# Attention over a key/value window plus a gated feed-forward block: block transposes written in order, strided reading by TensorE, masks and gathers put off by a tile

## The chip, the cores and the metric

The kernel runs on one core of a Trainium2 chip. The metric is the time of the whole kernel on the device in microseconds (us), the median of several runs. A core has TensorE (matrix products, written PE in the profile, its weight loads PEld), VectorE (DVE), ScalarE (ACT), GpSimd (POOL) and SyncE (SP), which here issues the large loads. Data lie in SBUF, an on-chip memory of 128 partitions, and matrix products land in PSUM.

## The reference

For two sequences (B = 2) of one new token each, the kernel normalises the token x and adds three things: x, attention over the last W = 4096 keys and values of a cache, and a feed-forward block with a rectified gate. All data are float32.

```python
W = min(4096, max(256, Sk // 4))                 # Sk = 32768
q = (xn @ wq).reshape(B, Sq, Hq, Dh)...          # Hq = 32 query heads, Dh = 128
k = repeat(k_cache[:, :, Sk - W:, :], rep)       # 8 key/value heads, rep = 4
scores = einsum("bhqd,bhkd->bhqk", q, k) * (Dh ** -0.5)
o = einsum("bhqk,bhkd->bhqd", softmax(scores), v)
attention = o.reshape(B, Sq, Hq * Dh) @ wo
gate, up = xn @ W_gate, xn @ W_up                # 512 x 1792 each
block = ((gate * (gate > 0)) * up) @ W_down
return x + attention + block
```

Each key and each value is used by four query heads only, so the work is mostly moving 95 MB from memory and bringing the keys into a shape that TensorE can multiply.

## The kernel before

**Tiles.** The 16 pairs of sequence and key/value head are worked on in four rows of heads (g = 0 to 3, the loop at the end of the planned part), each in two tiles (a = 0, 1). A tile is one 4 MB load of 128 partitions: two heads, 64 partitions each, with 64 keys of 128 numbers in every partition. Keys arrive as `k`, values as `v`. All large loads go through one ring of four buffers of 4 MB (`RING`, `load`), and SyncE issues them in the order of the code. A load waits until the tile that held its buffer four loads earlier has been used up, and every load behind it in SyncE's queue waits with it. The order of loads is wq (2), w_gate, w_up, the keys of row 0, and then, for g = 1 to 3 and a = 0, 1, the keys of (g, a) and the values of (g - 1, a); at the end the values of row 3, w_down and wo.

**Order of the work.** Nothing is planned by a program: every engine works in the order in which the code issues its instructions, and waits there for what it needs. While row g is scored, the values of row g - 1 are multiplied.

- `scores(g, a, kt_in)`: VectorE turns the keys so that the 128 numbers of a key lie along partitions. It transposes blocks of 32 x 32 within a tile, four instructions of 128 x 2048 elements for each tile of keys, two for each half s1 of the tile, written to a `kT` tile. There are two `kT` buffers. A block transpose leaves two heads interleaved in every 32 columns (index h), and the kernel before lets VectorE separate them: in the stream of results h runs fastest, while in `kT` [CB, 2, JH, KL] the two values of h lie 512 floats apart. TensorE then multiplies a 32-column strip of the queries `qz` with 512 columns of `kT`, one matmul for each of four groups of 32 numbers (cb) and each h; the output `s` has four strips of 32 partitions, one for each pair of s1 and h.
- `maxima(g)` (second tile only): the largest score of each head, over VectorE, a transpose on TensorE (`mt`), VectorE, and a matmul (`nm_ps`) that spreads it again to `nm`.
- `softmax`: ScalarE's exponential `p` with row sums `l`. `turn`: two matmuls `pp` permute `p`, VectorE transposes it to `pt`, and the reciprocals `rl` of the sums are made.
- `values(g, a, v)`: 16 matmuls in four strips give `o`; VectorE multiplies `o` with a mask (`on`), since only some of its blocks are wanted.
- `gather(g, a)`: one matmul collects the wanted heads in `oa`. `finish(g)`: VectorE sums (`su`) and scales (`osb`). `spread_heads(r)`: eight matmuls `op` and a copy to `oT` bring the heads of two rows into the shape for the last product.

After the rows come the values of row 3, then the products with w_down and wo (`y`, `y_ps`) and the output `yo`. Ahead of the rows stand the normalisation, the queries (`q_ps`, `qt`, `rq`, `qz`) and the gate (`g_ps`, `u_ps`, `hh`, `hT`).

Of the kernel before, what the change touches and what calls it, by code (L numbers as in the profile page):

```python
# [9 lines left out]
F32 = mybir.dt.float32  # L10
AF = mybir.ActivationFunctionType
ALU = mybir.AluOpType
# [8 lines left out]
def kernel(  # L21
# [13 lines left out]
    P = 128  # L35
    B, _, D = x.shape
    _, HKV, SK, DH = k_cache.shape
# [12 lines left out]
    S1 = W // (Q * 512)  # L50
    L = 32
    PB = P // L
    CB = DH // L
# [9 lines left out]
    ktp = ctx.enter_context(tc.tile_pool(name="ktp", bufs=2))  # L63
# [36 lines left out]
    def load_kv(cache, name, g, a):  # L100
        r, b = divmod(g, B)
        base = cache[b, r * C + a, SK - W:SK, :]
        run = J * DH
        src = bass.AP(
            tensor=cache.tensor, offset=base.offset, ap=[[run, PK], [NP * SK * DH, 2], [1, run]]
        )
        return load(f"{name}{g}_{a}", src, [P, run])
# [20 lines left out]
    qz = const.tile([P, NG, CB, 2, ZW], F32, name="qz")  # L128
# [26 lines left out]
    mask = const.tile([P, 4], F32, name="mask")  # L155
# [52 lines left out]
    for kc in range(KC):  # L208
        m, k = divmod(kc, 2)
# [17 lines left out]
    for r in range(R):  # L227
# [15 lines left out]
        for b in range(B):  # L243
            for pb in range(PB):
                rows = slice(L * pb, L * pb + L)
                for a in range(NP):
                    lo = 2 * a * 16 + pb * REP
# [33 lines left out]
    JH = J // S1  # L281
    KL = L // 2
    ss, pts, rls = {}, {}, {}
    osb, ons, oa = {}, {}, {}

    def scores(g, a, kt_in):
        if a == 0:
            ss[g] = ps_s.tile([P, 512], F32, name=f"s{g}", tag="s")
        for s1 in range(S1):
            kt = ktp.tile([P, CB, 2, JH, KL], F32, name=f"kT{g}_{a}_{s1}", tag="kT")  # L290
            for n in range(2):
                lo = JH // 2 * n
                j = JH * s1 + lo
                nc.vector.transpose(  # L294
                    kt[:, :, :, lo:lo + JH // 2, :].rearrange("p c h j k -> p j c k h"),
                    kt_in[:, j * DH:(j + JH // 2) * DH],
                )
            for cb in range(CB):
                for h in range(2):
                    lo = 32 * (2 * s1 + h)  # L300
                    nc.tensor.matmul(  # L301
                        ss[g][lo:lo + 32, :], qz[:, g, cb, h, 16 * a:16 * a + 32],
                        kt[:, cb, h].rearrange("p j k -> p (j k)"),
                        start=(a == 0 and cb == 0), stop=(a == NP - 1 and cb == CB - 1),
                    )

    def maxima(g):

        m = work.tile([P, 1], F32, name=f"m{g}", tag="m")
        nc.vector.tensor_reduce(out=m, in_=ss[g], op=ALU.max, axis=AX.X)  # L310
        mt = ps_1.tile([1, P], F32, name=f"mt{g}", tag="misc")
        nc.tensor.transpose(mt, m, ident)
        mx = work.tile([1, C, REP], F32, name=f"mx{g}", tag="mx")
        nc.vector.tensor_reduce(
            out=mx, in_=mt.rearrange("p (s x b i) -> p x i s b", s=S1, x=C, b=PB), op=ALU.max, axis=AX.XY
        )
        mb = work.tile([1, S1, C, PB, REP], F32, name=f"mb{g}", tag="mb")
        for s1 in range(S1):
            nc.vector.tensor_scalar(
                mb[:, s1], mx[:, :, None, :].to_broadcast([1, C, PB, REP]), -SCALE, None, op0=ALU.mult  # L320
            )
        nm_ps = ps_1.tile([P, 1], F32, name=f"nm_ps{g}", tag="misc")
        nc.tensor.matmul(nm_ps, mb.rearrange("p s x b i -> p (s x b i)"), ones, start=True, stop=True)
        nm = work.tile([P, 1], F32, name=f"nm{g}", tag="nm")
        nc.vector.tensor_copy(nm, nm_ps)  # L325
        return nm

    def softmax(g, nm):
        p = work.tile([P, 512], F32, name=f"p{g}", tag="p", bufs=1)
        l = work.tile([P, 1], F32, name=f"l{g}", tag="l")  # L330
        nc.scalar.activation(p, ss[g], AF.Exp, bias=nm, scale=SCALE, accum_out=l)  # L331
        return p, l

    def turn(g, p, l):
        pp = ps_kt.tile([P, 2, 512], F32, name=f"pp{g}", tag="kt")
        for h in range(2):
            nc.tensor.matmul(pp[:, h], perm[:, h], p, start=True, stop=True)  # L337
        pts[g] = work.tile([P, NP * S1, JH, HK], F32, name=f"pt{g}", tag="pt")
        nc.vector.transpose(pts[g].rearrange("p n j k -> p j n k"), pp.rearrange("p h y -> p y h"))  # L339
        lp = ps_1.tile([HR, 1], F32, name=f"lp{g}", tag="misc")  # L340
        nc.tensor.matmul(lp, by_h.rearrange("p x i -> p (x i)"), l, start=True, stop=True)
        rls[g] = work.tile([HR, 1], F32, name=f"rl{g}", tag="rl")
        nc.vector.reciprocal(rls[g], lp)

    def values(g, a, v):
        o = ps_1.tile([P, 512], F32, name=f"o{g}_{a}", tag="o")
        for s1 in range(S1):
            for jh in range(2):
                for q in range(Q):
                    j = 16 * jh + 4 * q  # L350
                    lo = (JH * s1 + j) * DH
                    nc.tensor.matmul(  # L352
                        o[32 * q:32 * q + 32, :], pts[g][:, a * S1 + s1, j:j + 4, :].rearrange("p u k -> p (u k)"), v[:, lo:lo + 512],
                        start=(s1 == 0 and jh == 0), stop=(s1 == S1 - 1 and jh == 1),
                    )
        ons[a] = work.tile([P, 4, P], F32, name=f"on{g}_{a}", tag="on")
        nc.vector.tensor_tensor(  # L357
            ons[a], o.rearrange("p (u d) -> p u d", u=4), mask[:, :, None].to_broadcast([P, 4, P]), op=ALU.mult
        )

    def gather(g, a):

        if a == 0:
            oa[g] = ps_1.tile([HR, 4, P], F32, name=f"oa{g}", tag="oa")
        nc.tensor.matmul(  # L365
            oa[g], picks[:, a].rearrange("p h a i -> p (h a i)"), ons[a], start=(a == 0), stop=(a == NP - 1)
        )

    def finish(g):
        r, b = divmod(g, B)  # L370
        if b == 0:
            osb[r] = const.tile([HR, B, P], F32, name=f"osb{r}")
        su = work.tile([HR, P], F32, name=f"su{g}", tag="su", bufs=1)
        nc.vector.tensor_reduce(out=su, in_=oa[g].rearrange("h u d -> h d u"), op=ALU.add, axis=AX.X)  # L374
        nc.vector.tensor_scalar(osb[r][:, b], su, rls[g], None, op0=ALU.mult)

    def spread_heads(r):
        op = ps_1.tile([P, NJ, B], F32, name=f"op{r}", tag="misc")
        for e in range(NE):
            nc.tensor.matmul(  # L380
                op, spread[:, e].rearrange("h k e -> h (k e)"),
                osb[r][:, :, e * NJ:(e + 1) * NJ].rearrange("h b j -> h j b"),
                start=(e == 0), stop=(e == NE - 1),
            )
        nc.vector.tensor_copy(oT[:, r, :, :, 0], op)

    for g in range(NG):
        for a in range(NP):
            kt_in = load_kv(k_cache, "k", g, a)
            v_in = load_kv(v_cache, "v", g - 1, a) if g else None  # L390
            scores(g, a, kt_in)
            nm = maxima(g) if a else None
            if g:
                values(g - 1, a, v_in)
            pl = softmax(g, nm) if a else None
            if g:
                gather(g - 1, a)
                if a:
                    finish(g - 1)
                elif g % B == 1 and g > 1:  # L400
                    spread_heads((g - 2) // B)
            if a:
                turn(g, *pl)
    g = NG - 1
    vin = [load_kv(v_cache, "v", g, a) for a in range(NP)]
    dw = load_down()
# [28 lines left out]
    for a in range(NP):  # L435
        values(g, a, vin[a])
        gather(g, a)
# [48 lines left out]
```

## Time and profile before

| | |
|---|---|
| median of 3 runs | 278.11 us (277.75 to 278.12) |
| profiled execution | 277.64 us, span 275.9 us |
| TensorE busy | 166.6 us (60%), 948 records |
| VectorE busy | 147.2 us (53%), 121 instructions |
| ScalarE, GpSimd busy | 8.3 us, 8.1 us |
| read from memory | 94.90 MB, 344 GB/s over the span |
| mean granted TensorE clock | 0.85 |

The profile is of one execution. The span is the time between its first and last instruction. A row of a group of instructions names line, engine, operation, output<-inputs and count, then the busy time in us with the mean length in ns, and after the second bar the idle time of the engine before them with what ended it. The chain is the sequence of work that ended last, followed back from the end: its pieces give start, length and what was done ("issue" is a short time in which nothing shown was waited for). A row of a window gives for each engine its busy time and instructions, then the granted clock as a share of full speed, the busy share of the DMA engines and GB/s. A float32 matmul appears as two records.

### The profile page before, as it was taken

To read this page: it belongs to the slowest core of one execution; us is meant where nothing else is said; L and a number is where in the kernel's file an instruction comes from. 1 tells how busy PE (TensorE), PEld (TensorE's weight loads), DVE (VectorE), ACT (ScalarE), POOL (GpSimd) and SP (SyncE) were. 2 spreads that over 40 slices of the span, in tenths; PEclk is the share of its full clock that TensorE was granted. 3 is DMA by queue.
4 is the path that set the end of the run, shared out by engine and by line. 5 is a ranking of instruction groups with operands and counts; after the bars stand their busy time and mean duration, and the time that the engine had idled before them with its cause. 6 is when DMAs were issued, how large, how long until landed. Compare 5 with 4: busy or idle time off the path is not lost.

```text
span 275.9 us, 2205 instructions
## 1 busy us (share of the span) xinstructions
PE 166.6 (60%) x948; PEld 51.7 (19%) x948; DVE 147.2 (53%) x121; ACT 8.3 (3%) x27; POOL 8.1 (3%) x31
## 2 busy tenths in 40 slices
PE   0049759158476079547642981777089617768894
PEld 0042342111111012011110120122012301212242
DVE  1030123899952993695269729923991398241201
ACT  0010112000001000000100000010000000100000
POOL 8200000000000000000000000000000000000000
PEclk9999968859898559959995797799759957999999
DMA  7999999999999905996996289799907992999940
GB/s 304 456 404 451 399 451 420 456 418 418 450 423 413 456 14 219 404 442 249 437 394 290 76 378 442 323 380 375 432 29 287 399 451 102 391 363 399 393 186 1
DMA packets 3784, 95.03 MB, mean 344 GB/s; under 512 B 438, under 2 KB 448, under 8 KB 704
## 3 DMA queue, kind: packets, MB, share of 16 engines
q1 hardware_dynamic: 3756, 94.90, 82.2%
q8 instruction: 7, 0.11, 0.2%
q14 instruction: 1, 0.01, 0.0%
q10 hardware_dynamic: 20, 0.00, 0.0%
HBM read 94.90 MB, written 0.00 MB: 344 GB/s over the span
## 4 chain that ended last, share of the span: by engine, by line
DVE 48%; PE 41%; issue 6%; POOL 3%; ACT 1%; POOLq 0%; ACTq 0%
DVE kT L294 40%; PE o L352 10%; PE s L301 9%; PE q_ps L221 3%; PE pp L337 3%; PE y L424 3%; PE oa L365 2%; DVE pt L339 2%; PE g_ps L258 2%; DVE on L357 2%; PE op L380 1%; PE xt_ps L211 1%; PE u_ps L258 1%; PE rq L239 1%; DVE m L310 1%
## 5 line engine op out<-in xcount | busy, mean ns | idle before, releaser
L301 PE MATMUL s<-kT,qz 128*32 128x512 f32 x256 | 77.3, 760 | 66.1 <-DVE kT L294 66.1
L294 DVE STREAM_TRANSPOSE kT<-k 128x2048 f32<-128x2048 f32 x32 | 115.6, 3722 | 0.0
L301 PEld LDWEIGHTS s<-kT,qz 128*32 128x32 f32 x256 | 16.5, 134 | 122.7 <-DVE kT L294 77.7
L352 PE MATMUL o<-v,pt 128*32 128x512 f32 x256 | 34.8, 595 | 0.0
L357 DVE TENSOR_TENSOR on<-o,mask 128x512 f32<-128x512 f32 x8 | 5.5, 692 | 40.4 <-PE o L352 40.4
L211 PE MATMUL xt_ps<-rep,xn 2*128 2x32 f32 x16 | 3.7, 400 | 17.4 <-DVE xn L205 17.4
L352 PEld LDWEIGHTS o<-v,pt 128*32 128x32 f32 x256 | 9.1, 109 | 16.6 <-issue 16.6
L365 PE MATMUL oa<-on,picks 128*16 128x512 f32 x16 | 8.3, 597 | 6.5 <-DVE on L357 6.5
L310 DVE TENSOR_REDUCE m<-s 128x1 f32<-128x512 f32 x4 | 2.8, 692 | 14.9 <-PE s L301 14.9
L337 PE MATMUL pp<-p,perm 128*128 128x512 f32 x16 | 9.1, 699 | 1.2 <-ACT p L331 1.2
L221 PE MATMUL q_ps<-wq,xnT 128*32 128x512 f32 x64 | 9.2, 738 | 0.5 <-DVE xnT L213 0.5
L339 DVE STREAM_TRANSPOSE pt<-pp 128x1024 f32<-128x1024 f32 x4 | 5.0, 1250 | 7.0 <-PE pp L337 7.0
L331 ACT ACTIVATE p<-s,nm 128x512 f32<-128x512 f32 x4 | 2.7, 687 | 191.8 <-DVE nm L325 191.8
L188 DVE BATCH_NORM_STATS2 stats<-x 2x6 f32<-2x512 f32 x1 | 0.7, 682 | 11.6 <-DMA x<-in_A_x_dram 11.6
L211 PEld LDWEIGHTS xt_ps<-rep,xn 2*128 2x128 f32 x16 | 3.6, 319 | 17.4 <-issue 17.4
L248 DVE COPY qz<-rq 32x32 f32<-32x32 f32 x16 | 3.0, 187 | 7.1 <-ACT qz L248 7.1
L236 DVE COPY qT<-qt 128x32 f32<-128x32 f32 x2 | 0.4, 192 | 11.1 <-PE qt L232 11.1
L424 PE MATMUL y<-wo,oT 128*32 128x512 f32 x48 | 5.4, 594 | 0.0
L374 DVE TENSOR_REDUCE su<-oa 16x128 f32<-16x512 f32 x4 | 2.7, 679 | 4.5 <-PE oa L365 4.5
L258 PE MATMUL g_ps<-wg,xnT 128*32 128x448 f32 x32 | 4.5, 717 | 0.0
L424 PE MATMUL y<-wd,hT 128*32 128x512 f32 x28 | 4.5, 595 | 0.0
L232 PE MATMUL qt<-ident,qs 128*128 128x128 f32 x8 | 1.7, 357 | 4.4 <-DVE qs L229 4.4
(79 smaller groups left out, 67.9 us busy)
## 6 DMA issues: line engine op xcount, KB each, us to landing
k<-in_A_k_cache_dram SPq DMA_DIRECT2D x8, 4096.0 KB, 17.7
v<-in_A_v_cache_dram SPq DMA_DIRECT2D x8, 4096.0 KB, 16.7
wq<-in_A_wq_dram SPq DMA_DIRECT2D x2, 4096.0 KB, 16.8
wo<-in_A_wo_dram SPq DMA_DIRECT2D x1, 4096.0 KB
wg<-in_B_W_gate_dram SPq DMA_DIRECT2D x1, 3584.0 KB
wu<-in_B_W_up_dram SPq DMA_DIRECT2D x1, 3584.0 KB
wd<-in_B_W_down_dram SPq DMA_DIRECT2D x1, 3584.0 KB, 10.9
wo<-in_A_wo_dram SPq DMA_DIRECT2D x1, 2048.0 KB
```

What stands on the lines that cost most here:

```text
L211: nc.tensor.matmul(xt_ps[:, o, kc, :], cols, rep.rearrange("r s b -> r (s b)"), start=True, stop=True)
L221: nc.tensor.matmul(q_ps[r][32 * c:32 * c + 32, :], xnT[:, 0, kc, :], wqt[kc // 2][:, kc % 2, n * 512:(n + 1) * 512], start=(kc == 0), stop ...
L258: nc.tensor.matmul(dst[32 * c:32 * c + 32, :], xnT[:, 1, kc, :], wt[:, kc, c * MQ:(c + 1) * MQ], start=(kc == 0), stop=(kc == KC - 1),)
L294: nc.vector.transpose(kt[:, :, :, lo:lo + JH // 2, :].rearrange("p c h j k -> p j c k h"), kt_in[:, j * DH:(j + JH // 2) * DH],)
L301: nc.tensor.matmul(ss[g][lo:lo + 32, :], qz[:, g, cb, h, 16 * a:16 * a + 32], kt[:, cb, h].rearrange("p j k -> p (j k)"), start=(a == 0 an ...
L310: nc.vector.tensor_reduce(out=m, in_=ss[g], op=ALU.max, axis=AX.X)
L337: nc.tensor.matmul(pp[:, h], perm[:, h], p, start=True, stop=True)
L339: nc.vector.transpose(pts[g].rearrange("p n j k -> p j n k"), pp.rearrange("p h y -> p y h"))
L352: nc.tensor.matmul(o[32 * q:32 * q + 32, :], pts[g][:, a * S1 + s1, j:j + 4, :].rearrange("p u k -> p (u k)"), v[:, lo:lo + 512], start=(s ...
L357: nc.vector.tensor_tensor(ons[a], o.rearrange("p (u d) -> p u d", u=4), mask[:, :, None].to_broadcast([P, 4, P]), op=ALU.mult)
L365: nc.tensor.matmul(oa[g], picks[:, a].rearrange("p h a i -> p (h a i)"), ons[a], start=(a == 0), stop=(a == NP - 1))
L424: nc.tensor.matmul(y4[32 * t:32 * t + 32, :], lhsT.rearrange("p b s -> p (b s)"), w, start=(i < Q), stop=(i >= EARLY - Q))
```

## The change

Four things change in the functions of the rows.

1. `kT` is now [JH, CB, KL, 2], the order in which the transpose delivers its results, so VectorE writes one float behind the other. The heads stay interleaved, and the matmuls read every second float of `kT` (`kts[s1][:, :, cb, :, h]`).
2. The matmuls of a tile of keys are issued after both halves have been transposed, with the halves s1 inside the loop over cb: four strips in turn where there were two. Both `kT` buffers are therefore held until the 16 matmuls are nearly over.
3. The mask moves from `values` into `gather`, and `gather`, `finish` and `spread_heads` go to a list `late`, which is worked off in the next tile of keys, behind the transposes of its first half.
4. Exponential and `turn` come ahead of `values` in the second tile of a row.

```diff
-            kt = ktp.tile([P, CB, 2, JH, KL], F32, name=f"kT{g}_{a}_{s1}", tag="kT")
+            kt = ktp.tile([P, JH, CB, KL, 2], F32, name=f"kT{g}_{a}_{s1}", tag="kT")
+            kts.append(kt)
             for n in range(2):
...
                 nc.vector.transpose(
-                    kt[:, :, :, lo:lo + JH // 2, :].rearrange("p c h j k -> p j c k h"),
+                    kt[:, lo:lo + JH // 2].rearrange("p j c k h -> p (j c k h)"),
                     kt_in[:, j * DH:(j + JH // 2) * DH],
                 )
-            for cb in range(CB):
+            while late:
+                late.pop(0)()
+        for cb in range(CB):
+            for s1 in range(S1):
                 for h in range(2):
                     lo = 32 * (2 * s1 + h)
                     nc.tensor.matmul(
-                        ss[g][lo:lo + 32, :], qz[:, g, cb, h, 16 * a:16 * a + 32],
-                        kt[:, cb, h].rearrange("p j k -> p (j k)"),
+                        ss[g][lo:lo + 32, :], qz[:, g, cb, h, 16 * a:16 * a + 32], kts[s1][:, :, cb, :, h],
...
-        ons[a] = work.tile([P, 4, P], F32, name=f"on{g}_{a}", tag="on")
-        nc.vector.tensor_tensor(
-            ons[a], o.rearrange("p (u d) -> p u d", u=4), mask[:, :, None].to_broadcast([P, 4, P]), op=ALU.mult
-        )
-
-    def gather(g, a):
+        os[a] = o
+
+    def gather(g, a):
+
+        ons[a] = work.tile([P, 4, P], F32, name=f"on{g}_{a}", tag="on")
+        nc.vector.tensor_tensor(
+            ons[a], os[a].rearrange("p (u d) -> p u d", u=4), mask[:, :, None].to_broadcast([P, 4, P]), op=ALU.mult
+        )
...
             scores(g, a, kt_in)
-            nm = maxima(g) if a else None
+            if a:
+                turn(g, *softmax(g, maxima(g)))
             if g:
                 values(g - 1, a, v_in)
-            pl = softmax(g, nm) if a else None
-            if g:
-                gather(g - 1, a)
+                late.append(lambda g=g, a=a: gather(g - 1, a))
                 if a:
-                    finish(g - 1)
+                    late.append(lambda g=g: finish(g - 1))
                 elif g % B == 1 and g > 1:
-                    spread_heads((g - 2) // B)
-            if a:
-                turn(g, *pl)
+                    late.append(lambda g=g: spread_heads((g - 2) // B))
+    while late:
+        late.pop(0)()
```

Two places in the order of instructions show it. First VectorE, from the end of row 1 to the first mask of row 2; `kT_0_0` is the half s1 = 0 of tile a = 0, `on_1` the mask product of the second tile of the row before. Before:

```order
L325 COPY nm_483<-nm_ps_481 128x1
L357 TENSOR_TENSOR on_1_502<-o_1_485,mask 128x512
L374 TENSOR_REDUCE su_509<-oa_444 16x128
L375 TENSOR_SCALAR osb_508<-su_509,rl_396 16x128
L339 STREAM_TRANSPOSE pt_515<-pp_512 128x32x4x8
L343 RECIPROCAL rl_519<-lp_517 16x1
L294 STREAM_TRANSPOSE kT_0_0_526<-k_0_521 128x16x4x16x2 x2
L294 STREAM_TRANSPOSE kT_0_1_537<-k_0_521 128x16x4x16x2 x2
L357 TENSOR_TENSOR on_0_565<-o_0_548,mask 128x512
```

And after the change:

```order
L331 COPY nm_483<-nm_ps_481 128x1
L345 STREAM_TRANSPOSE pt_491<-pp_488 128x32x4x8
L349 RECIPROCAL rl_495<-lp_493 16x1
L298 STREAM_TRANSPOSE kT_0_0_519<-k_0_514 128x2048 x2
L367 TENSOR_TENSOR on_1_522<-o_1_497,mask 128x512
L382 TENSOR_REDUCE su_526<-oa_451 16x128
L383 TENSOR_SCALAR osb_525<-su_526,rl_396 16x128
L298 STREAM_TRANSPOSE kT_0_1_529<-k_0_514 128x2048 x2
L298 STREAM_TRANSPOSE kT_1_0_569<-k_1_565 128x2048 x2
```

The mask and the head sum of row 0 have moved from ahead of `pt` to between the two halves of the next tile of keys, and the first mask of row 2's tile has moved on by half a tile.

Second TensorE, the same stretch: the end of row 1 and the first tile of row 2. Before:

```order
L323 MATMUL nm_ps_481<-ones,mb_478 128x1
L352 MATMUL o_1_485<-v_1_448,pt_392 32x512 x16
L365 MATMUL oa_444<-on_1_502,picks 16x512
L337 MATMUL pp_512<-p_504,perm 128x512 x2
L341 MATMUL lp_517<-l_505,by_h 16x1
L301 MATMUL s_525<-kT_0_0_526,qz 32x512 x8
L301 MATMUL s_525<-kT_0_1_537,qz 32x512 x8
L352 MATMUL o_0_548<-v_0_523,pt_515 32x512 x16
```

And after the change:

```order
L329 MATMUL nm_ps_481<-ones,mb_478 128x1
L343 MATMUL pp_488<-p_485,perm 128x512 x2
L347 MATMUL lp_493<-l_486,by_h 16x1
L358 MATMUL o_1_497<-v_1_444,pt_392 32x512 x16
L373 MATMUL oa_451<-on_1_522,picks 16x512
L308 MATMUL s_518<-kT_0_0_519,qz 32x512 x2
L308 MATMUL s_518<-kT_0_1_529,qz 32x512 x2
L308 MATMUL s_518<-kT_0_0_519,qz 32x512 x2
L308 MATMUL s_518<-kT_0_1_529,qz 32x512 x2
```

The values and the gather have moved behind `pp`, and the score matmuls alternate between the two halves, where one half was finished before the other began.

More of the change, by code (lines that the diff above doesn't have):

```diff
@@ L283 @@
     ss, pts, rls = {}, {}, {}
-    osb, ons, oa = {}, {}, {}
+    osb, os, ons, oa = {}, {}, {}, {}
+    late = []
     def scores(g, a, kt_in):
@@ L288, in scores @@
             ss[g] = ps_s.tile([P, 512], F32, name=f"s{g}", tag="s")
+        kts = []
         for s1 in range(S1):
-            kt = ktp.tile([P, CB, 2, JH, KL], F32, name=f"kT{g}_{a}_{s1}", tag="kT")
+            kt = ktp.tile([P, JH, CB, KL, 2], F32, name=f"kT{g}_{a}_{s1}", tag="kT")
+            kts.append(kt)
             for n in range(2):
```

## The prediction

> **What bounds the kernel now.** I read the page first: the head, the slices, the chain by line.
>
> ```profile
> span 275.9 us, 2205 instructions
> ...
> DMA  7999999999999905996996289799907992999940
> ...
> DVE kT L294 40%; PE o L352 10%; PE s L301 9%; PE q_ps L221 3%; PE pp L337 3%; PE y L424 3%; PE oa L365 2%; DVE pt L339 2%; PE g_ps L258 2%; DVE on L357 2%; PE op L380 1%; PE xt_ps L211 1%; PE u_ps L258 1%; PE rq L239 1%; DVE m L310 1%
> ```
>
> Forty per cent of the chain is one line, the block transposes of the keys. DMA runs full for the first third and then has holes. Next the chain in order of time (start, length, what): pieces of row 0 of the four rows of heads, then row 2 whole, from the end of one pt to the end of the next.
>
> ```profile
> 50.87 9.45 DVE kT L294 x3
> ...
> 85.83 0.79 ACT p L331 x2
> 86.62 0.14 issue
> 86.75 3.21 PE pp L337 x4
> ...
> 91.27 14.39 DVE kT L294 x4
> ...
> 142.43 14.39 DVE kT L294 x4
> ...
> 160.50 3.46 PE o L352 x26
> 164.01 0.57 issue
> 164.59 14.48 DVE kT L294 x4
> ...
> 179.11 3.65 PE s L301 x16
> 182.79 0.70 DVE m L310
> ...
> 184.94 3.62 PE o L352 x32
> 188.57 0.70 DVE on L357
> ...
> 189.32 1.03 PE oa L365 x2
> 190.35 1.93 PE pp L337 x4
> 192.31 1.25 DVE pt L339
> ...
> 193.59 14.38 DVE kT L294 x4
> ```
>
> Nothing overlaps at the seams: VectorE transposes, TensorE multiplies scores and then values, VectorE masks, and only then come the next keys. A row takes 193.59 - 142.43 = 51.2 us. The loads wait for this chain, not the reverse, as SyncE's queue and the DMA windows show.
>
> ```profile
> SPq L73 <- DVE kT L294: 120.5, 7, 25.3
> ...
> 45.00:95.00 50.00, 26.60 (x133) 7.17 (x125) 37.60 (x23) 1.28 (x3) 0.00 (x0) 0.79 1.01 432
> ...
> 150.00:155.00 5.00, 5.00 (x14) 1.11 (x12) 5.00 (x2) 0.00 (x0) 0.00 (x0) 0.50 0.00 0
> ```
>
> SyncE waits 120.5 us for transposes to free ring slots. DMA sustains 432 GB/s where it isn't held up (last column) and moves nothing at 150 to 155 us.
>
> **The change part by part.**
>
> *In-order writes.* The 32 transposes and their nearest relations on VectorE:
>
> ```profile
> L294 DVE STREAM_TRANSPOSE kT<-k 128x2048 f32<-128x2048 f32 x32 | 115.6, 3722 | 0.0
> L339 DVE STREAM_TRANSPOSE pt<-pp 128x1024 f32<-128x1024 f32 x4 | 5.0, 1250 | 7.0 <-PE pp L337 7.0
> L267 DVE TENSOR_TENSOR hh<-gr,u_ps 128x448 f32<-128x448 f32 x1 | 0.9, 911 | 1.8 <-PE u_ps L258 1.8
> L357 DVE TENSOR_TENSOR on<-o,mask 128x512 f32<-128x512 f32 x8 | 5.5, 692 | 40.4 <-PE o L352 40.4
> L374 DVE TENSOR_REDUCE su<-oa 16x128 f32<-16x512 f32 x4 | 2.7, 679 | 4.5 <-PE oa L365 4.5
> L375 DVE TENSOR_SCALAR osb<-su,rl 16x128 f32<-16x128 f32 x4 | 1.1, 274 | 0.1
> L456 DVE COPY yo<-y_ps 128x128 f32<-128x128 f32 x1 | 0.3, 291 | 2.3 <-PE y_ps L431 2.3
> ```
>
> The kT transpose costs 1.82 ns an element; consecutive results go 2 KB apart (h is innermost in the stream and strides 512 floats). The pt transpose, which writes runs of 8 floats, costs 1.22. The product hh, written 32 floats apart, takes 2.03 an element against 1.35 for the product on, written in order. So the scattered write is the excess. Price in order: the copy yo of 128 elements and the product on of 512 give a slope of (692 - 291)/384 = 1.044 ns and 157 ns fixed, hence 157 + 2048 x 1.044 = 2.30 us. Ends: 2.14 (slope alone) and 3.72 (nothing won); at the pt rate it would be 2.50. I take 2.30, since pt by the same line gives 1.23 against 1.25 measured. Saved: 32 x 1.42 = 45 us of VectorE.
>
> *Strided reading and four strips at once.* Before, eight matmuls of one kT tile use two strips of 32 columns (two h); after, 16 matmuls cycle over four strips (two s1, two h), as the values matmuls do. Rows at full clock, and the same batch when the clock is low:
>
> ```profile
> 127.95 3.63 PE L301 MATMUL s<-kT,qz 128*32 128x512 f32 x16 [1.54 <-DVE kT L294]
> 133.70 3.64 PE L352 MATMUL o<-v,pt 128*32 128x512 f32 x32
> 149.67 6.55 PE L301 MATMUL s<-kT,qz 128*32 128x512 f32 x16 [8.43 <-DVE kT L294]
> ```
>
> Each matmul leaves two records, so two strips need 3.63 us for 8 and four strips 3.64 us for 16. In-order data would thus give 3.64 us per 16-matmul batch at full clock. What reading every second float does to it, no row shows. Lowest end: nothing (a stride doesn't shorten reading). The other end is the only matmul with a strided moving operand and many columns, the head spreading (32 columns, 512 bytes apart in b):
>
> ```profile
> 216.91 1.91 PE op L380 x16
> ```
>
> That is 0.24 us for each of 8 matmuls, hence at most 7.5 ns a column, 3.8 us for 512 columns, 15.2 us per batch if four share it. Most of that row is weight loading, so I take no price and keep the upper end for the rivals. [...]
>
> *The clock.* A batch now starts after both kT tiles, so TensorE idles longer before it. Windows of 1 us (first the busy time of TensorE; the last three columns are granted clock, DMA share, GB/s):
>
> ```profile
> 114.00:115.00 1.00, 0.59 (x2) 0.00 (x0) 1.00 (x1) 0.00 (x0) 0.00 (x0) 1.00 0.83 360
> ...
> 118.00:119.00 1.00, 0.00 (x0) 0.00 (x0) 1.00 (x1) 0.00 (x0) 0.00 (x0) 0.53 1.21 524
> ...
> 120.00:121.00 1.00, 0.24 (x2) 0.19 (x4) 1.00 (x2) 0.00 (x0) 0.00 (x0) 0.50 0.76 328
> ...
> 124.00:125.00 1.00, 1.00 (x6) 0.22 (x4) 1.00 (x2) 0.00 (x0) 0.00 (x0) 0.56 1.20 508
> ```
>
> The clock fell to 0.50 about 3.4 us after the last matmul (114.6 to 118) and came back 4.1 us after work resumed (120.8 to 124.9). The batch at 149.67 took 6.55 us instead of 3.63, so some 5.8 us of it were at half clock. With the mean, 5.0 us, 2.5 us of the 3.64 are done at half clock and 1.1 remain: a cold batch lasts 6.1 us. The last TensorE work before a batch is the put-off gather, some 3.5 us earlier where no head sum follows, over 5 us where one does, so I expect most batches cold: S = 5.6 us in the mean (3.64 and 7.28 are the ends). [...]
>
> *Values, mask and gather off VectorE's path.* Before, the next transposes wait for the values (3.46 + 0.57 in the first tile of a row, 3.62 + 0.70 + 1.03 in the second). After, values run beside the next tile's first two transposes (4.6 us against 3.64), and the mask and gather come behind these. The cover is needed: were it gone, 3.64 comes back per tile. The masks stay on VectorE (0.70 each). The head sum stands between transposes and waits there for its gather: 1.03 + 0.68 + 0.27 = 2.0 us in the first tile of rows 2 and 3, formerly beside pp; the head spreading in row 3 makes VectorE wait 1.03 + 1.91 = 2.9. The transposes queued behind these wait with them. From score end to pt end: 2.15 (182.79 to 184.94), then exp, no longer covered by values, 0.79 + 0.14 (row 0 has it bare), pp 1.93, pt 1.25, 0.04: R = 6.3 us. The values of the second tile come 3 us later than before, and with them the freed ring slot; that load's predecessor is then still on its way, so I cost it at nothing. SyncE's order of loads and POOL's work don't change.
>
> *The sum.* VectorE can't start the next keys before the batch has freed both kT buffers, so transposes and batches add up. Row 0 starts at 50.87 as now: 2 x (9.2 + 6.1) + 7.5 (R with pp at half clock) = 38.1, end 89.0 (91.3 before). Row 1: eight transposes 18.4, one mask 0.7, two batches 11.2, R 6.3: 36.6. Row 2: one mask and the head sum more, 39.3. Row 3: the spreading more, 42.2. The last pt ends at 207.1. Loads need 16.8 MB a row, 39.0 us at 432 GB/s, so they nearly set the pace too. Tail:
>
> ```profile
> 247.97 0.18 DVE y_ps L410
> ...
> 248.60 3.61 PE o L352 x32
> ```
>
> Before, the last pt ended at 247.9, and the values of row 3's first tile at 252.2. Now the last values of row 2 come first, 3.64 from 206.3 on; then mask 0.75, gather 1.03, head sum 0.95, y_ps with its clearing 0.6 (247.97 to 248.60), and the values of row 3's first tile 3.64, to 216.9. Everything behind keeps its distance: 275.9 - (252.2 - 216.9) = 240.6. The profiled execution took 277.64, 1.74 over its span, and the median of the runs is 0.47 above that: 243 us.
>
> **Rivals.**
> - *The loads bind.* With a warm clock (S = 3.64) the rows shrink below 39 us and 94.9 MB at 432 GB/s from 1.5 us on end at 221; with the 10 us that now follow the last load (the DMA slices end in 4 and 0, 6.9 us each) the span is 231, the time 233.5. For: 39.0 is close to my rows. Against: the clock rows.
> - *Strided reading costs up to double.* A full-speed batch of 7.28, S = 9.3: 8 x 3.7 = 30 more, 273. For: no row of strided reading; against: nothing but the unknown. Half that price gives 258.
> - *Slower: strided reading costs more.* It decides from 35.3 / 8 = 4.4 us per batch on, a matmul quartet 2.2 times as long as the contiguous one; at the upper end, 15.2 us per batch, 8 x 11.6 = 93 more, 336. For: four strips read at once, which doubles the demand that two made. Against: most of the row op is weight loading.
> - *The change doesn't do what it says.* Transposes stay at 3.72 because something other than the scattered write holds them: 45 back, 288, slower, as batches now stand bare behind them. Against: pt and hh.
>
> **How the numbers follow.** Forecast 0.66, loads 0.09, strided reading up to 2.2 times 0.11, beyond it 0.08, transposes unchanged 0.06. Faster by over 0.2% (about what a measurement can tell here) is the first three, 0.86; of the two others 0.01 falls where they happen to meet the old time: 0.86, 0.01, 0.13. The forecast's own range is 234 to 257: S from 4.6 to 6.6 (8 us either way), transposes up to 2.50 (6 more). The whole range, 232 to 266, takes in the load bound and most of the third case and leaves out some 0.18.
>
> **What would show it.** Transposes at 2.2 to 2.5 us; a 16-matmul score batch of 3.6 us at clock 1.00 and about 6 at first 0.50; no values or mask ahead of transposes in the chain; DMA slices full to the end. Transposes near 3.7, or a warm batch over 4 us, would make me wrong; so would SyncE waits for values of tens of us.

## The result

The changed kernel takes 236.78 us (median of 4 runs, 235.44 to 237.79) against 278.12 us before: ratio 0.850 (95% interval 0.844 to 0.856). 243 us had been forecast, with a range of 232 to 266. The profiled execution took 236.89 us. Where an execution was over 1.5% slower than the fastest of its kernel, the time given is the median of the others.

First the page of the kernel after: span, DMA slices, the chain by line.

```profile
span 235.1 us, 2205 instructions
...
DMA  7999999999999999899999999999999999989950
...
DVE kT L298 29%; PE s L308 15%; PE pp L343 5%; PE o L358 5%; PE q_ps L221 4%; PE y L431 4%; PE oa L373 3%; DVE on L367 2%; PE g_ps L258 2%; PE op L388 2%; DVE pt L345 2%; PE xt_ps L211 2%; PE u_ps L258 1%; ACT p L337 1%; PE rq L239 1%
```

The transposes still lead the chain, with 29% of 235 us instead of 40% of 276. The holes in the DMA slices are gone, although no load is on the chain. Then the groups of instructions:

```profile
L298 DVE STREAM_TRANSPOSE kT<-k 128x2048 f32<-128x2048 f32 x32 | 71.5, 2278 | 18.3 <-PE s L308 18.3
L308 PE MATMUL s<-kT,qz 128*32 128x512 f32 x256 | 53.1, 786 | 41.1 <-DVE kT L298 41.1
L358 PE MATMUL o<-v,pt 128*32 128x512 f32 x256 | 35.6, 647 | 0.0
L343 PE MATMUL pp<-p,perm 128*128 128x512 f32 x16 | 12.2, 906 | 4.7 <-ACT p L337 4.7
```

One transpose takes 2278 ns instead of 3722, and VectorE now idles 18.3 us for scores that hold the kT buffers. A matmul of pp has become longer, 906 ns against 699. The chain in order of time shows one row of heads, row 1 (start, length, what):

```profile
87.06 4.41 DVE kT L298 x2
91.50 4.35 DVE kT L298 x2
95.86 0.04 issue
95.90 4.51 PE s L308 x22
100.44 4.50 DVE kT L298 x2
104.94 0.58 DVE on L367
105.52 4.42 DVE kT L298 x2
109.93 0.04 issue
109.98 3.76 PE s L308 x27
113.76 0.70 DVE m L316
...
116.20 0.79 ACT p L337 x2
116.99 0.04 issue
117.03 3.79 PE pp L343 x4
120.85 1.25 DVE pt L345
122.14 4.40 DVE kT L298 x2
```

In row 1 values and gather no longer stand in the chain; the mask does. A row that took 51.2 us takes 35.1 here, and 37.7 and 41.2 in rows 2 and 3, which begin at 122.14 and 159.88.

### The profile page after: what moved, and what is told of

Read it like the earlier page. It is cut to its first block, busy times and chain, and to the rows that moved or that the text cites. A ratio compares the mean times of both kernels' runs of the same rounds, so it can differ in the third digit from the quotient of the medians.

```text
span 235.1 us, 2205 instructions
## 1 busy us (share of the span) xinstructions
PE 145.4 (62%) x948; PEld 48.0 (20%) x948; DVE 102.5 (44%) x121; ACT 8.3 (4%) x27; POOL 8.1 (3%) x31
## 4 chain that ended last, share of the span: by engine, by line
PE 47%; DVE 40%; issue 6%; POOL 3%; ACT 2%; POOLq 0%; ACTq 0%; DVEq 0%
DVE kT L298 29%; PE s L308 15%; PE pp L343 5%; PE o L358 5%; PE q_ps L221 4%; PE y L431 4%; PE oa L373 3%; DVE on L367 2%; PE g_ps L258 2%; PE op L388 2%; DVE pt L345 2%; PE xt_ps L211 2%; PE u_ps L258 1%; ACT p L337 1%; PE rq L239 1%
## 5 line engine op out<-in xcount | busy, mean ns | idle before, releaser
L298 DVE STREAM_TRANSPOSE kT<-k 128x2048 f32<-128x2048 f32 x32 | 71.5, 2278 | 18.3 <-PE s L308 18.3
L308 PE MATMUL s<-kT,qz 128*32 128x512 f32 x256 | 53.1, 786 | 41.1 <-DVE kT L298 41.1
L358 PE MATMUL o<-v,pt 128*32 128x512 f32 x256 | 35.6, 647 | 0.0
L308 PEld LDWEIGHTS s<-kT,qz 128*32 128x32 f32 x256 | 11.0, 135 | 76.4 <-DVE kT L298 51.1
L343 PE MATMUL pp<-p,perm 128*128 128x512 f32 x16 | 12.2, 906 | 4.7 <-ACT p L337 4.7
L358 PEld LDWEIGHTS o<-v,pt 128*32 128x32 f32 x256 | 10.6, 119 | 18.6 <-issue 18.6
L221 PE MATMUL q_ps<-wq,xnT 128*32 128x512 f32 x64 | 10.0, 792 | 0.5 <-DVE xnT L213 0.5
L343 PEld LDWEIGHTS pp<-p,perm 128*128 128x128 f32 x16 | 3.7, 256 | 8.0 <-issue 4.2
```

Source lines behind the costliest of these rows:

```text
L221: nc.tensor.matmul(q_ps[r][32 * c:32 * c + 32, :], xnT[:, 0, kc, :], wqt[kc // 2][:, kc % 2, n * 512:(n + 1) * 512], start=(kc == 0), stop ...
L298: nc.vector.transpose(kt[:, lo:lo + JH // 2].rearrange("p j c k h -> p (j c k h)"), kt_in[:, j * DH:(j + JH // 2) * DH],)
L308: nc.tensor.matmul(ss[g][lo:lo + 32, :], qz[:, g, cb, h, 16 * a:16 * a + 32], kts[s1][:, :, cb, :, h], start=(a == 0 and cb == 0), stop=(a ...
L358: nc.tensor.matmul(o[32 * q:32 * q + 32, :], pts[g][:, a * S1 + s1, j:j + 4, :].rearrange("p u k -> p (u k)"), v[:, lo:lo + 512], start=(s ...
```

## The experiments

Each run is compared with the kernel before on the same chip. That kernel's median lay between 278.1 and 279.6 us, so the ratio to it is given beside each time. In the diffs "..." marks what is left out. Theory A: the chain of VectorE and TensorE sets the time. Theory B: the loads do.

**layout_only.** The first part of the change alone, on the kernel before.

```diff
-            kt = ktp.tile([P, CB, 2, JH, KL], ...)
+            kt = ktp.tile([P, JH, CB, KL, 2], ...)
...
-                    kt[:, :, :, lo:lo + JH // 2, :].rearrange("p c h j k -> p j c k h"),
+                    kt[:, lo:lo + JH // 2].rearrange("p j c k h -> p (j c k h)"),
...
-                        kt[:, cb, h].rearrange("p j k -> p (j k)"),
+                        kt[:, :, cb, :, h],
```

> The kernel before with the first part of the change alone: transposes write in order, the matmuls read every second float; two strips, masks and values stand where they stood. Theory A (the chain of VectorE and TensorE sets the time): 32 transposes are 1.44 us shorter, 46 us, but the cold 8-matmul batch of the first half (6.5 us) no longer fits beside the second half's transposes (4.4 us) and gives about 2 us per tile back: 278 - 46 + 16 = 248 us, range 242 to 254. Theory B (the loads set the time after the change): this part alone already reaches them, 235 to 238 us, as the changed kernel.

Measured: 239.15 us, ratio 0.856 (0.854 to 0.858). The interval overlaps that of the whole change, so this part alone brings nearly all or all of the gain. Theory A's 248 (242 to 254) was a miss. Theory B's 235 to 238 came closer, but not for its reason: no load is on the chain of this kernel. The chain of this kernel for row 2:

```profile
124.23 4.41 DVE kT L294 x2
128.65 0.04 issue
128.69 7.13 PE s L301 x26
...
137.27 3.45 PE o L352 x24
140.78 0.57 issue
141.36 4.50 DVE kT L294 x2
145.86 0.04 issue
145.91 8.37 PE s L301 x32
154.30 0.70 DVE m L310
```

From the end of the first half's transposes both batches together take 8.4 us, so they end 4.0 us after the second half's transposes, not 5.7: adding a whole cold batch (6.5 us) to a whole warm one (3.65) was too much. The second half's transposes have left the chain, and TensorE's scores have taken their place.

**order_only.** The other parts without the layout: the changed kernel with the two lines of the layout undone.

```diff
-            kt = ktp.tile([P, JH, CB, KL, 2], ...)
+            kt = ktp.tile([P, CB, 2, JH, KL], ...)
...
-                    kt[:, lo:lo + JH // 2].rearrange("p j c k h -> p (j c k h)"),
+                    kt[:, :, :, lo:lo + JH // 2, :].rearrange("p c h j k -> p j c k h"),
...
-                        ... kts[s1][:, :, cb, :, h],
+                        ... kts[s1][:, cb, h].rearrange("p j k -> p (j k)"),
```

> The changed kernel with the old layout of kT: scattered writes, contiguous reads, but four strips and the put-off work. Theory A: each of 32 transposes stands bare in the chain, 1.44 us longer: 236.8 + 46 = 283 us, slower than before by 5 us. If the order of work were what hides the transposes, it would stay under 250.

Measured: 290.66 us, ratio 1.040 (1.038 to 1.042), almost 8 us above Theory A's number but on its side. The groups of this kernel:

```profile
L298 DVE STREAM_TRANSPOSE kT<-k 128x2048 f32<-128x2048 f32 x32 | 116.5, 3723 | 19.9 <-PE s L308 19.9
L308 PE MATMUL s<-kT,qz 128*32 128x512 f32 x256 | 65.6, 935 | 67.6 <-DVE kT L298 67.6
```

Only the layout changed, and a transpose is back at 3723 ns: the scattered write is the cause of its length. The new order alone makes the kernel slower: both halves' transposes stand ahead of the scores, and these transposes, which had waited for nothing before the change, wait 19.9 us for scores. The score matmuls also became longer (935 ns against the changed kernel's 786), with a mean granted clock of 0.77 against 0.855.

**two_strips.** The changed kernel, each half's matmuls again right behind its transposes.

```diff
             while late:
                 late.pop(0)()
-        for cb in range(CB):
-            for s1 in range(S1):
+            for cb in range(CB):
                 for h in range(2):
...
-                        ... kts[s1][:, :, cb, :, h],
+                        ... kt[:, :, cb, :, h],
```

> The changed kernel with each half's eight matmuls right behind its transposes, two strips at a time, as before. Theory A: the first half's batch runs beside the second half's transposes and wakes the clock, the second takes 3.65 us at full clock where the changed kernel's batch takes 4.6 in the mean after the last transpose; against it the spill of a cold first batch, 6.5 - 4.4 = 2.1. Time 233 to 240 us, so four strips gain next to nothing. Rival: four strips are worth what they halve, 8 x 3.65 = 29 us, 260 us or more.

Measured: 230.30 us (230.01 to 230.94), ratio 0.824 (0.823 to 0.825): faster than both kernels, 3% under the changed one by the ratios, and 2.7 us below Theory A's range. Issuing the matmuls of both halves together, in four strips, is not a gain but a loss. Its chain by line, and the transposes' group with what VectorE waited for:

```profile
DMA k<-in_A_k_cache_dram 24%; DVE kT L296 15%; PE s L305 11%; PE o L355 7%; PE q_ps L221 4%; PE y L428 4%; PE g_ps L258 3%; PE pp L340 3%; PE op L385 2%; PE oa L370 2%; DVE on L364 2%; PE xt_ps L211 2%; PE u_ps L258 1%; PE rq L239 1%; PE y_ps L435 1%
L296 DVE STREAM_TRANSPOSE kT<-k 128x2048 f32<-128x2048 f32 x32 | 71.5, 2278 | 12.0 <-DMA k<-in_A_k_cache_dram 9.5 <-PE s L305 2.5
```

The wait for scores has shrunk from 18.3 to 2.5 us, and 9.5 us of waiting for keys have come instead: this kernel runs into the loads.

**not_late.** The changed kernel with nothing put off.

```diff
-                late.append(lambda g=g, a=a: gather(g - 1, a))
+                gather(g - 1, a)
                 if a:
-                    late.append(lambda g=g: finish(g - 1))
+                    finish(g - 1)
                 elif g % B == 1 and g > 1:
-                    late.append(lambda g=g: spread_heads((g - 2) // B))
+                    spread_heads((g - 2) // B)
```

> The changed kernel with mask, gather, head sum and spreading at once behind the values, so VectorE waits for the values ahead of the next transposes. Theory A: 3.64 us for values and 0.5 for the rest come back in each of the five tiles that have a next one: 236.8 + 5 x 4.1 = 257 us, range 250 to 260. Theory B: the loads cover this, under 241 us.

Measured: 262.77 us, ratio 0.940 (0.937 to 0.942): Theory A, and 3 us above its range. The chain at the end of row 1:

```profile
113.00 6.29 PE s L308 x28
...
122.58 3.78 PE pp L343 x4
126.37 0.12 PE lp L347
126.48 4.65 PE o L358 x29
131.15 0.70 DVE on L367
131.86 0.04 issue
131.90 1.05 PE oa L373 x2
132.97 0.69 DVE su L382
133.68 0.28 DVE osb L383
133.96 8.81 DVE kT L298 x4
```

Values, mask, gather and head sum are back between pp and the next transposes, and the batch takes 6.29 us where the changed kernel's takes 3.76: TensorE, which in the changed kernel does values and gather beside the transposes, has only two early score matmuls to do beside them here, and the batch runs at a granted clock of 0.50 from 113 to 118 us.

**layout_four and two_not_late** fill the table. The first is layout_only with four strips: the edit of two_strips is made the other way round, so both halves are transposed and then come the loops cb, s1, h. The second is two_strips with the edit of not_late.

> In-order writes and strided reading as in layout_only, and four strips after both halves; masks, values and exponential where the kernel before has them. If the first half's batch beside the second half's transposes is what layout_only lives on: after the first half's transposes layout_only needs about 8.3 us to the end of the scores, this one 4.4 for transposes and about 5.0 for a cold batch of 16, so some 1.2 us more in each of 8 tiles, 239.2 + 10 = 249 us. If four strips gain anything by themselves: under 239.

> The two_strips kernel with nothing put off; beside layout_only it differs in the exponential and turn ahead of the values alone. Expected: the exponential is bare (0.9 us), pp runs at low clock (3.8 instead of 1.9), and the head sum loses its cover (1.0), some 4 us in each of three rows: 239.2 + 12 = 251 us. Then putting off is worth 20 us with either order of strips. If putting off is worth little with two strips: under 240.

Measured: layout_four 254.49 us, ratio 0.913 (0.907 to 0.919), dearer than expected; two_not_late 246.91 us, ratio 0.885 (0.880 to 0.890), between the two expectations and nearer to the first. The chain of layout_four, to be held against that of layout_only:

```profile
131.61 8.80 DVE kT L296 x4
140.41 0.04 issue
140.45 5.65 PE s L304 x25
...
146.59 3.46 PE o L354 x28
```

From the first transpose of the tile until TensorE has only values left 15.0 us pass here (131.61 to 146.59), there 13.0 (124.23 to 137.27). In the eight tiles the difference is 1.1 to 2.4 us, 14 in all, which is about the 15 that four strips cost. These edits change two things at once, the strips in turn and the wait for both halves. The rows of the prediction have 8 matmuls in two strips at 3.63 us and 16 in four at 3.64, so the turn itself costs TensorE nothing, and the wait is left; no run separates the two.

| all with the in-order layout (us, ratio) | two strips | four strips |
|---|---|---|
| exponential behind values, nothing put off | 239.15, 0.856 | 254.49, 0.913 |
| exponential ahead of values, nothing put off | 246.91, 0.885 | 262.77, 0.940 |
| exponential ahead, masks and gathers put off | 230.30, 0.824 | 236.78, 0.850 |

Read downwards, the early exponential alone costs 8 us, and putting off gives 17 or 26 back; together the two gain 9 us with two strips and 18 with four. The chain of two_not_late shows the cost: the exponential is bare (0.79 us), pp takes 3.6 us in rows 1 and 2 where it takes 1.9 in layout_only, and the head sum is uncovered (1.0 us). No run puts work off with the exponential behind the values. Then the values would stand ahead of pp in TensorE's queue, so the early exponential may be what putting off needs, and no loss; that is argued from the order of the code and not shown. Read across, four strips cost 15, 16 and 6.5 us. The change is a large gain from the layout (40 us), a smaller one from the early exponential and putting off together, and a loss from four strips that eats most of the latter.

**half_v, no_max and half_v_no_max** ask what sets the time of the changed kernel. The first halves the values' bytes, the second leaves out the largest scores.

```diff
+        got = run // 2 if name == "v" else run
-            ... ap=[[run, PK], [NP * SK * DH, 2], [1, run]]
+            ... ap=[[run, PK], [NP * SK * DH, 2], [1, got]]
...
-                    lo = (JH * s1 + j) * DH
+                    lo = j * DH
```

```diff
-        m = work.tile([P, 1], F32, name=f"m{g}", tag="m")
...
-        nc.vector.tensor_copy(nm, nm_ps)
+        nc.vector.memset(nm, 0.0)
```

> The changed kernel with every load of values halved (the matmuls use the first half's values twice): 16.8 MB, about 39 us of loading, less; no instruction of VectorE or TensorE changes. Theory A (chain): 235 to 237 us, as the changed kernel. Theory B (loads): 200 to 215 us.

> The changed kernel without the largest scores (the shift of the exponential is the constant zero, so reductions, transpose and spreading fall away): about 2.3 us less in the chain of each of four rows. Theory A: 236.8 - 9 = 228 us, but not below the loads, which need 94.9 MB at 422 GB/s, 225 us, and 10 us behind them: so 233 to 236 us, and DMA as full as before. Theory B: 236.8, no change.

> Both at once: half of the values' bytes and no largest scores. Theory A: the chain without its floor, 236.8 - 9 = 228 us. Theory B (loads): 200 to 215 us, as with the half values alone.

Measured: half_v 235.99 us, ratio 0.845 (0.839 to 0.851); no_max 230.35, ratio 0.826 (0.821 to 0.832); both together 226.50, ratio 0.811 (0.804 to 0.818). Taking away a sixth of the bytes does nothing, taking 2.3 us a row off the chain does much: Theory A, though the changed kernel's DMA engines are as busy as they look. First the changed kernel's whole stretch of loading (DMA share and GB/s last), then the DMA slices of half_v, then the chain by line of no_max:

```profile
2.00:226.00 224.00, 140.10 (x852) 45.41 (x856) 100.72 (x115) 8.32 (x27) 6.71 (x25) 0.85 0.99 422
```

```profile
DMA  7999999999999980499964699992864787289940
```

```profile
DVE kT L298 28%; PE s L308 19%; DMA wo<-in_A_wo_dram 8%; PE o L343 5%; PE q_ps L221 4%; PE pp L328 3%; PE oa L358 3%; PE g_ps L258 2%; DVE on L352 2%; PE xt_ps L211 2%; PE u_ps L258 1%; ACT p L322 1%; PE rq L239 1%; PE y_ps L423 1%; DVE su L367 1%
```

In half_v the holes are back and the time stays. In no_max a load, that of wo, comes onto the chain, and some 4 us are lost to the loads, as the run with both edits shows. The loads' floor thus lies at about 230 us, not at the 233 to 236 expected. What no_max takes off the chain is a net: without the maxima pp takes 2.0 us in rows 1 and 2 instead of 3.8, but the batch of row 1's second tile takes 5.4 instead of 3.8.

**two_half_v.** The two_strips kernel with the edit of half_v.

> The two_strips kernel with half of the values' bytes. Its chain shows waits for the keys, so the loads should bind there: with 16.8 MB less it falls to what its VectorE and TensorE need, some 226 to 229 us. If the loads don't bind: 230.3 us unchanged.

Measured: 226.89 us (225.08 to 227.54), ratio 0.812 (0.807 to 0.817). So the loads hold two_strips up, for some 3 us.

**read_runs and read_runs16** price the strided reading.

```diff
-                        ... kts[s1][:, :, cb, :, h],
+                        ... kts[s1][:, 16 * h:16 * h + 16, cb, :, :].rearrange("p j k h -> p j (k h)"),
```

```diff
-                        ... kts[s1][:, :, cb, :, h],
+                        ... kts[s1][:, :, cb, 8 * h:8 * h + 8, :].rearrange("p j k h -> p j (k h)"),
```

> The changed kernel with as many moving columns of kT, but in runs of 32 consecutive floats (half of the keys for both heads) instead of every second float: the price of strided reading alone. If it costs nothing: 236 to 237.5 us and a full-clock batch of 14 matmuls as long as now, 3.73 us. If it costs something, each 10% of a batch is 0.36 us, 8 x 0.36 = 3 us.

> The changed kernel with runs of 16 consecutive floats of every block (half of the numbers twice over, for both heads) instead of every second float, and with the same dependence on both transposes of a half: the price of strided reading, which read_runs mixed with an earlier start. If the stride costs nothing: 236 to 237.5 us; if it costs the 0.1 us that separates 3.73 from 3.63 in a batch: 0.8 us less, 235.5 to 236.5, hardly to be told apart; under 234 would be a price of over 0.3 us a batch.

Measured: read_runs 232.80 us, ratio 0.832 (0.824 to 0.840), scattered from 230.1 to 233.2. Some 4 us under the changed kernel would by its expectation be a price of over 10% of a batch. But it answers something else: its matmuls need one transpose of a half each and begin earlier. read_runs16, without that flaw, takes 235.56 us (235.12 to 237.68), ratio 0.846 (0.841 to 0.850), not to be told from the changed kernel. The same 14 matmuls at full clock, first in the changed kernel, then in read_runs16 (timeline of TensorE):

```profile
109.98 3.73 PE L308 MATMUL s<-kT,qz 128*32 128x512 f32 x28 [2.51 <-DVE kT L298]
```

```profile
108.48 3.63 PE L308 MATMUL s<-kT,qz 128*32 128x512 f32 x28 [2.52 <-DVE kT L298]
```

The stride costs 0.10 us in this batch, 3%. The other batch at full clock, in row 2, takes 3.79 against 3.63 us.

## Why the prediction was right, point by point

- **In-order writes at 2.30 us.** Right: 2.28 us, and order_only shows that the scattered write was the excess. The line through two other VectorE instructions carried over to the transpose; that it came within 1% is partly luck, since those are other operations.
- **Strided reading at nothing.** Right but for 3 to 4% of a batch. No row before the change showed the stride by itself. Taking no price was my estimate, from a row op in which the weight loads are busy for 1.86 of 1.97 us (the kernel before, at 216.84); read_runs16 shows what it costs: 3.73 us with the stride against 3.63 without. The two rivals that hung on a price did not come.
- **The batch of scores, S = 5.6 us.** Mis-sized: the eight pieces of the chain after the last transpose of a tile are 4.9, 5.6, 4.5, 3.8, 4.3, 3.8, 4.3 and 5.2 us, 4.6 in the mean, the lowest that my range allowed. Six of the eight batches began at a granted clock of 0.50, so "most batches cold" held. Three things were missed.
  First, the second tiles of rows 1 and 2 ran at full clock. There values, gather and the first two score matmuls, which need the first half's transposes alone, keep TensorE at work until 107.5, 2.5 us ahead of the batch; I had reckoned with 3.5 us and left those two matmuls out.
  Second, a cold batch was shorter than the 6.1 us forecast. The granted clock was back 2.8 to 4.0 us after its start, not 5.0, and to its last matmul it lasted 5.1 to 5.6 us.
  Third, in the first tile of a row VectorE goes on 0.7 to 0.9 us before the last matmul ends, because only the first half's buffer has to be free by then.
  All batches together came out 9.4 us shorter than forecast, more than the 5.5 us by which the whole span did; the next point gives a part back. The clock coming back in the batch that begins at 95.90 (granted clock third from the end):

```profile
98.00:99.00 1.00, 1.00 (x8) 0.19 (x4) 0.00 (x0) 0.00 (x0) 0.00 (x0) 0.50 0.91 360
99.00:100.00 1.00, 1.00 (x12) 0.23 (x8) 0.00 (x0) 0.00 (x0) 0.00 (x0) 0.89 0.82 328
```

- **From score end to pt end, R = 6.3 us.** Mis-sized the other way: 8.4 us in rows 1 and 2 (113.76 to 122.14), 7.3 in row 3, and 6.6 in row 0, where 7.5 had been forecast: 4.3 us more over the four rows. I priced the exponential that values no longer cover, but not the clock there: in row 1 TensorE works for 0.6 of the 3.3 us between the batch and pp (113.7 to 117.0), the granted clock falls from 1.00 to 0.50 in the last microsecond of them, and in rows 1 and 2 pp runs at 0.50 (3.8 us for the 1.93 forecast). The windows of the changed kernel, one around a second tile's batch, one around pp of row 2:

```profile
105.00:110.00 5.00, 1.92 (x10) 0.40 (x10) 4.92 (x3) 0.00 (x0) 0.00 (x0) 1.00 0.94 380
155.00:160.00 5.00, 5.00 (x14) 1.40 (x18) 1.41 (x3) 0.00 (x0) 0.00 (x0) 0.50 1.00 433
```

- **Values, mask and gather.** Right: values run beside transposes, the head sum holds VectorE 2.1 us (127.1 to 129.2 in row 2), the spreading in row 3 stops it 3.2 where 2.9 were forecast.
- **The rows and the tail.** Forecast 38.1, 36.6, 39.3 and 42.2 us, measured 34.9, 35.1, 37.7 and 41.2; they begin 1.3 us later than before, and the tail is 34.0 us long against 33.5. What is left of the difference is in transposes, which follow one another at 2.2 us, some 3 us less in all.
- **The loads bind.** Not in this kernel (half_v), but nearly, some 6 us away (no_max, two_strips). The floor of 233.5 us was put 3 us too high.
- **The signs.** One sign of being wrong was no sign. SyncE's waits for values came to 54.6 us in five waits, tens of us as named, but they had been 37.3 before, and the DMA slices are full all the same: SyncE waits for a slot while earlier loads are still on their way.
- **What the sum didn't ask.** It took the parts of the change together. It did count that transposes and batches add up, but counted four strips as neutral and never priced the change without them. It compared only the batch, 3.64 us in two strips for half the work or in four for all; the cost is the cover that the first half's batch loses. The early exponential was counted, but without the clock. That the forecast came within 6 us is partly luck: batches 9.4 us too long and transposes some 3 too long stood against 4.3 us missing from score end to pt end.

## What to carry to other kernels

When a write pattern makes an engine's longest instruction slow, try it the other way round, with the writer in order and the reader strided; here, where the reader takes every second float, the exchange rate was 1.44 us saved for each of 32 transposes against 0.1 to 0.2 us for each of 8 batches. Packing more matmuls side by side was worth nothing here, where it made them wait for an input that could have been prepared beside them (layout_four 254.49 us, layout_only 239.15). Split a change that bundles several orders before judging it: here the layout brings 40 us, the early exponential and putting off together 9 to 18, and the four strips take 6.5 to 15 away, which the total hid.

## What the runs showed that was not expected

- Work put beside the transposes also kept TensorE's clock up in this kernel. Behind values, gather and two early score matmuls the batch of row 1's second tile took 3.8 us at a granted clock of 1.00; where values and gather were done ahead of the transposes and only the two early matmuls beside them (not_late), the same batch took 6.3, mostly at 0.50.
- DMA engines busy 99% of a stretch at 422 GB/s are no proof that loads bind: with 16.8 MB fewer the changed kernel took as long as with them (half_v, 235.99 us against 236.78).
- Removing the largest scores and changing the strips, two unrelated edits, end at the same 230.3 us, each with a load on the chain, and go to 226.5 and 226.9 us when the values' bytes are halved.
